# Sliding-window attention with a gated MLP on one core: scores of three units in one tiling mode at the head of an exp phase, first masks as products, second q,k pieces issued early

## The chip, the cores and the metric

The kernel runs on one NeuronCore of one Trainium2 chip. The time is device time in microseconds (us) of that core. Before the change it is 304.06 us, the median of five runs (302.56 to 306.17).

## What is computed

Eight batches of eight heads, 576 tokens, head size 64. A query sees itself and the 127 tokens before it; each head subtracts its own slope times the distance from the scores (ALiBi). The result, as 4608 rows of 512, goes through two matrices with g = h * cos(h) between them.

```python
scores = scale * np.matmul(q, k.transpose(0, 1, 3, 2))
slopes = 2.0 ** (-8.0 * (np.arange(H, dtype=np.float32) + 1) / H)
bias = slopes[:, None, None] * (-np.abs(rel).astype(np.float32))[None, :, :]
mask = (rel >= 0) & (rel < window)
scores = np.where(mask, scores + bias[None], -1000000000.0)
...
return np.matmul(attn, v).astype(np.float32)
...
h = x @ w_in
g = h * np.cos(h)
return (g @ w_out).astype(np.float32)
```

Scale is 1/8, window 128, H is 8; attn is the softmax of the scores along the keys. x has 512 columns, w_in goes to 2048 and w_out back to 512.

## The kernel before

**Units.** Attention is cut into units. A unit (b, pr, G) is a pair of heads pr (of four) of batch b and 256 queries (G = 0 or 1); (b, "t", None) is the rest of 64 queries for all eight heads. A batch has nine units, all have 72. For a unit, TensorE (PE) makes the scores with 64 rows of the array for each of the two heads side by side (`scores`), ScalarE (ACT) takes the exponential out of PSUM (`exps`, L538, for tails L530), VectorE (DVE) multiplies by the mask, exp(slope * distance) inside the window and 0 outside (`mask`, L562 and L549, from the tile EM, that `masks` makes on ACT, L431, from the distances `dif`), PE multiplies by v with a column of ones for the sums (`pv`, L593 and L596, for tails L580 and L582), DVE divides (`norm`, one unit, L632 and L634; `norm_two`, two units at once, L647 and L649), and the result is transposed into xT, the input of the first matrix: on PE (`x_pe`, L700; `x_pe_two`, L662; a copy by ACT or DVE after it) or, if it is needed only after the next chunk, by a DMA of the SP queue (`x_dma`). `norm_two` is used where the two units of a group are neighbours in pr at an even count of units.

**Chunks.** The MLP goes over nine chunks c of 512 rows. `moe1` makes h in 16 pieces, each four matmuls into one PSUM bank (L738; for chunk 0 halves, `moe1_half`, L762), a cosine on ACT (L744) and a product on DVE (L748). `moe2` multiplies by w_out: for chunk 0 plainly (L823), for the others as seven products of half-size blocks with sums in place of the eighth (L879), whose results ACT and DVE take out of the banks (L899, L903). Cosine and exponential need different tables on ACT, so a stage alternates: cosines of chunk c, then an exp phase with the units of the quota of c, beside which PE runs moe2 of c.

**PSUM.** Eight banks: SB, banks 4 to 7, for scores in two slots of two; UB, banks 2 and 3, for PV; OB, banks 0 and 1, for moe2. While units remain, moe1 takes the six banks of UB + SB in turn. QUOTA says how many units each exp phase has; the first nine units go before chunk 0. `attention` takes units in groups of two. In the phases the scores of a group are one op (with `mode=1`), in the first attention each unit has its own. PV follows by group.

**Order.** `Plan.op` records every operation with what it reads and writes; waits between engines follow from that. The order on each engine is not found at run time: STARTS is a packed table with a start for every op and, for copies that either may do, the choice of ACT or DVE. `schedule` sorts by it. POOL's ops keep the order in which the program names them: its queue carries the loads that convert to bf16 (q and k, v, w_in, w_out), and `identity` and `distances` run on the same engine. A new table can therefore reorder all engines but POOL.

**Start.** The first pieces of q (SP queue, then a cast on DVE and ACT, L321 and L322) and k (POOL) cover the first 256 tokens, the second pieces (`load_qk("q", q, 0, 1)` and the same for k) the rest. `qk_transposes` brings them into place on PE (L451) with copies on ACT and DVE (L468, L469). `warm` and `keep` are matmuls whose results nobody reads (L416, L424). w_in comes in four quarters; unit f2 of `moe1_half` reads quarter f2 // 2.

The softmax here doesn't subtract the row's maximum and nothing guards it: scores larger than these inputs give would overflow.

## Time and profile before

The profiled execution took 302.56 us, its span from the first to the last instruction is 300.8 us. It is the fastest of the five.

| engine | busy us | share of the span | largest groups (line, count, us busy) |
|---|---|---|---|
| PE | 293.6 | 98% | L738 x576, 130.9; L879, four groups, 155.0 in sum |
| DVE | 244.3 | 81% | L748 x128, 83.0; L562 x96, 41.9; L634 x36, 14.3; L649 x14, 9.7 |
| ACT | 210.2 | 70% | L744 x128, 82.4; L538 x64, 55.6 |
| POOL | 94.9 | 32% | loads of v (L329 x40), q and k (L339 x60) |

Further rows that the prediction uses, as mean duration of one:

| row | count | mean ns |
|---|---|---|
| L506 and L497, scores (PE) | 320 and 128 | 239 and 191 |
| L632 and L634, reciprocal and product of one unit (DVE) | 36 each | 171 and 419 |
| L647 and L649, the same of two units (DVE) | 14 each | 205 and 690 |
| L662 and L700, transposes of x (PE) | 20 and 50 | 219 and 220 |
| L431, masks (ACT) | 8 | 403 |
| L468 and L469, copies of transposed q and k (ACT, DVE) | 8 and 8 | 754 and 779 |
| L899, copy of a product out of PSUM (ACT) | 18 into qrows | 550 |

How to read it: a matmul's duration holds its way through the array, and the next one starts long before it ends; what one costs is the step from its start to the next start. A group's idle time stands before its instructions, with what ended it. Landings of loads are those of their semaphores in the trace.

### The profile page before, as it was taken

The numbers are of one execution on the slowest core, as the hardware profiler recorded it, in microseconds if no ns is written. First come the engines' busy times: TensorE is split into PE (matmuls) and PEld (weight loads), VectorE is DVE, ScalarE is ACT, GpSimd is POOL, SyncE is SP. The second block draws the span as 40 slices with busy tenths as digits, with TensorE's granted clock in tenths as the row PEclk, the third lists the DMA queues.
The fourth block names the chain that finished last, engine by engine and source line by source line (L and its number), as shares of the span: only waits on it lengthen the run. The fifth ranks groups of instructions, "written<-read, shape, count | busy, mean of one in ns | idle before, by whom it ended". The sixth has DMA issues, their size and how long they took to land.

```text
span 300.8 us, 7152 instructions
## 1 busy us (share of the span) xinstructions
PE 293.6 (98%) x2917; PEld 199.7 (66%) x2917; DVE 244.3 (81%) x511; ACT 210.2 (70%) x304; POOL 94.9 (32%) x122
## 2 busy tenths in 40 slices
PE   7789999999999999999999999999999999999996
PEld 3478745546874588547898886468655865666685
DVE  3787898679977998899978989899887966886871
ACT  6877777487877686787768866788567955745431
POOL 6930992059958401870195014000000000000000
DMA  7999999999999999999599999747014004310123
GB/s 138 180 200 211 207 171 145 143 141 225 157 137 205 158 156 187 171 169 159 91 141 136 135 114 137 144 79 124 11 53 117 9 2 113 107 35 2 35 87 124
DMA packets 148064, 38.02 MB, mean 126 GB/s; under 512 B 133696, under 2 KB 146752, under 8 KB 148032
## 3 DMA queue, kind: packets, MB, share of 16 engines
q0 software_dynamic: 99344, 18.10, 76.5%
q1 hardware_dynamic: 48688, 19.47, 33.4%
q8 instruction: 23, 0.38, 0.5%
q14 instruction: 9, 0.07, 0.1%
HBM read 36.70 MB, written 9.44 MB: 153 GB/s over the span
## 4 chain that ended last, share of the span: by engine, by line
PE 92%; DMA 4%; POOL 1%; issue 1%; DVE 0%; ACT 0%; ACTq 0%
PE ps L738 37%; PE ps L879 33%; PE ps L823 5%; PE ps L506 5%; PE ps L762 4%; DMA w_inb<-in_moe_w_in_dram 3%; PE ps L593 3%; PE ps L596 2%; DMA ob<-in_q_dram 1%; POOL vp L329 1%; PE ps L451 1%; PE ps L497 1%; PE ps L700 1%; PE ps L580 1%; PE ps L582 1%
## 5 line engine op out<-in xcount | busy, mean ns | idle before, releaser
L738 PE MATMUL ps<-xT,w_inb 128*128 128x512 bf16 (+1 forms) x576 | 130.9, 355 | 0.0
L744 ACT ACTIVATE cos<-ps,halfpi 128x512 f32<-128x512 f32 x128 | 82.4, 688 | 39.9 <-PE ps L738 24.2
L748 DVE TENSOR_TENSOR gT<-ps,cos 128x512 f16<-128x512 f32 x128 | 83.0, 686 | 21.4 <-ACT cos L744 20.3
L738 PEld LDWEIGHTS ps<-xT,w_inb 128*128 128x128 bf16 x576 | 55.2, 98 | 39.7 <-DVE gT L748 2.0
L538 ACT ACTIVATE p<-ps 128x768 bf16<-128x768 f32 (+1 forms) x64 | 55.6, 915 | 10.9 <-PE ps L506 8.2
L329 POOL DMA_DIRECT2D vp<-in_v_dram x40 | 33.9, 880 | 67.8 <-PE ps L596 52.0
L879 PE MATMUL ps<-wsum,gT 128*128 128x256 f16 x256 | 48.8, 273 | 0.0
L562 DVE TENSOR_TENSOR p<-p,emask 128x512 bf16<-128x512 bf16 (+2 forms) x96 | 41.9, 460 | 3.5 <-ACT p L538 2.9
L879 PE MATMUL ps<-w_outb,gT 128*128 128x256 f16 x256 | 41.8, 273 | 0.0
L879 PE MATMUL ps<-wsum,gsum 128*128 128x256 f16 x256 | 38.2, 273 | 0.0
L339 POOL DMA_DIRECT2D qnat<-in_q_dram x30 | 25.4, 888 | 16.6 <-DMA qt<-qnat 16.0
L879 PEld LDWEIGHTS ps<-w_outb,gT 128*128 128x128 f16 x256 | 24.6, 98 | 8.3 <-issue 0.5
L879 PEld LDWEIGHTS ps<-wsum,gT 128*128 128x128 f16 x256 | 24.2, 98 | 7.3 <-issue 0.6
L879 PEld LDWEIGHTS ps<-wsum,gsum 128*128 128x128 f16 x256 | 24.5, 98 | 5.2 <-DVE ob L903 0.2
L339 POOL DMA_DIRECT2D knat<-in_k_dram x30 | 25.5, 918 | 5.1 <-issue 4.3
L879 PE MATMUL ps<-w_outb,gsum 128*128 128x256 f16 x128 | 26.2, 273 | 0.0
L506 PE MATMUL ps<-qt,kt 64*128 64x128 bf16 (+1 forms) x320 | 18.8, 239 | 0.9 <-DVE kt L469 0.6
L593 PEld LDWEIGHTS ps<-vp,p 128*128 128x128 bf16 x256 | 16.2, 98 | 5.0 <-issue 1.9
L593 PE MATMUL ps<-vp,p 128*128 128x65 bf16 x256 | 18.3, 193 | 0.9 <-DVE p L562 0.8
L899 ACT ACTIVATE qrows<-ps 128x512 f32<-128x512 f32 (+1 forms) x18 | 9.9, 550 | 12.3 <-PE ps L879 12.2
L596 PE MATMUL ps<-vp,p 128*128 128x65 bf16 x192 | 17.1, 193 | 0.0
L823 PE MATMUL ps<-w_outb,gT 128*128 128x512 f16 x64 | 16.9, 380 | 0.0
(80 smaller groups left out, 339.8 us busy)
## 6 DMA issues: line engine op xcount, KB each, us to landing
out_dram<-ob SPq DMA_DIRECT2D x32, 256.0 KB, 3.0
vp<-in_v_dram POOLq DMA_DIRECT2D x32, 128.0 KB, 8.5
qnat<-in_q_dram POOLq DMA_DIRECT2D x24, 128.0 KB, 10.2
knat<-in_k_dram POOLq DMA_DIRECT2D x24, 128.0 KB, 12.8
w_inb<-in_moe_w_in_dram POOLq DMA_DIRECT2D x4, 512.0 KB, 9.8
w_outb<-in_moe_w_out_dram POOLq DMA_DIRECT2D x4, 512.0 KB, 21.2
out_dram<-ob SPq DMA_DIRECT2D x8, 128.0 KB, 1.7
qrows<-in_q_dram POOLq DMA_DIRECT2D x1, 576.0 KB, 14.5
```

The costliest lines, as they stand in the source:

```text
L329: op("pool", [lambda e, t=t, rows=rows: e.dma_start(vp[b % 2][0:rows, t, :, 0:64], v[b, :, 128 * t:128 * t + rows, :].rearrange("h p d -> ...
L339: fns.append(lambda e, t=t, rows=rows: e.dma_start(nat[which][b % 2][0:rows, t, :, :], src[b, :, 128 * t:128 * t + rows, :].rearrange("h p ...
L506: ins = e.matmul(ps[:, banks[x], c0:c1], keys_ap(b, x, pr, kc), query_ap(b, x, pr, qb, 128 * nb), start=True, stop=True)
L538: op("act", lambda e: e.activation(P[i][:, :, 0:hi], src_[:, :, 0:hi], ACTF.Exp, scale=0.125), w=held + [("P", i)], occ=920 if G else 691, ...
L562: op("dve", lambda e, p=p, m=m: e.tensor_tensor(p, p, m, ALU.mult), r=[("P", i), ("EM", h0), ("EM", h1)], w=[("P", i)] if n != 1 else [("P ...
L593: ins = e.matmul(o, P[i][:, x, d0:d0 + 128], V[:, kc, h, 0:65], start=True, stop=not two)
L596: ins = e.matmul(o, P[i][:, x, p0:p0 + 128], V[:, kc - 1, h, 0:65], start=False, stop=True)
L738: op("pe", lambda e, kc=kc, c0=c0: e.matmul(ps[:, bank, c0:c0 + n], w_in[:, kc, 128 * fc:128 * fc + 128], xT[:, kc, (r0 + c0) % XR:(r0 + c ...
L744: op("act", lambda e: e.activation(cosb[ci][:, :], ps[:, bank, :], ACTF.Sin, bias=halfpi[:, 0:1]), r=["halfpi"], w=[("B", bank), ("cos", c ...
L748: op("dve", lambda e: e.tensor_tensor(gT[gi][:, fc, :], ps[:, bank, :], cosb[ci][:, :], ALU.mult), r=[("cos", ci)], w=[("B", bank), ("g", ...
L823: op("pe", lambda e, t=t, fc=fc, bank=bank: e.matmul(ps[:, bank, :], gT[gi][:, fc, 128 * t:128 * t + 128], w_out[:, fc, :], start=(fc == 0 ...
L879: op("pe", lambda e, t=t, fc=fc, bk=bk: e.matmul(ps[:, bk, 256 * t:256 * t + 256], lhs(fc, t), rhs(fc), start=first and fc == 0 and (last ...
```

## The change

Six things in one diff, and a new table STARTS, which is left out here.

- `scores` takes a list of bank pairs instead of a slot number. A third slot, UB, is added to the two of SB. In an exp phase with an odd number of units the first group has three units, whose scores are one op; later groups have two.
- `attention` keeps units whose scores are made in a list `waiting` and hands them to PV (`attend`) as neighbours (pr even, pr + 1) also across groups.
- QUOTA moves one unit from the fifth phase to the fourth, so all phases have an odd number.
- For the four units of G = 0 in the first attention, `biases` puts 8 * slope * distance into the banks by matmuls of a scaled identity with `dif`; the scores add to it, and the mask multiplication of these units goes. The eight scaled identities are made on DVE and lie in output buffer 2. `dif` becomes bf16.
- The second pieces of q and k are issued on POOL before `identity` and `distances`, whose order is swapped.
- `keep` has a count of 0, and the two `warm2` matmuls go.

```diff
@@ -262,15 +261,16 @@
         NOB = 4
         obuf = sb("ob", [128, NOB, 512], F32)
         ob = [obuf[:, i, :] for i in range(NOB)]
+        scaled = obuf[:, 2, :].bitcast(BF16).rearrange("p (h c) -> p h c", h=H)
         rec = [sb(f"rec{i}", [128, 8], F32) for i in range(2)]
         ident = sb("ident", [128, 128])
         halfpi = sb("halfpi", [128, 1], F32)
-        dif = sb("dif", [128, 2, 128], F32)
+        dif = sb("dif", [128, 2, 128])
 
         ps = ctx.enter_context(nc.psum_tensor("ps", [128, 8, 512], F32))
         BPE = 2
-        KEEP = 4
-        QUOTA = [9, 9, 11, 10, 10, 9, 5]
+        KEEP = 0
+        QUOTA = [9, 9, 11, 11, 9, 9, 5]
         SB, UB, OB = [4, 5, 6, 7], [2, 3], [0, 1]
 
         slopes = [2.0 ** (-8.0 * (h + 1) / H) for h in range(H)]
@@ -425,6 +425,36 @@
                     ps[:, OB[0], :], EM[:, 0, 0:128],
                     EM[:, 0:2, :].rearrange("p h c -> p (h c)"), start=True, stop=True),
                    r=[("EM", 0), ("EM", 1)], w=[("B", OB[0])], occ=213, lat=378, pri=0)
+
+        def scaled_identities():
+            for h in range(H):
+                op("dve", lambda e, h=h: e.tensor_scalar(
+                    scaled[:, h, :], ident[:, :], 8.0 * slopes[h], None, ALU.mult),
+                   r=["ident"], w=[("scaled", h)], occ=95, lat=180, pri=3)
+
+        def biases(u, banks):
+
+            b, pr, G = u
+
+            def f(e):
+                ins = None
+                if pr == "t":
+                    for k_ in range(NPAIR):
+                        for x in range(2):
+                            ins = e.matmul(ps[:, banks[x], 128 * k_:128 * k_ + 128],
+                                           scaled[:, 2 * k_ + x, :], dif[:, :, 0:64],
+                                           start=k_ == 0, stop=False, skip_group_check=True)
+                    return ins
+                for c0, n in ((0, 2), (256, 2 if G else 1)):
+                    for x in range(2):
+                        ins = e.matmul(ps[:, banks[x], c0:c0 + 128 * n], scaled[:, 2 * pr + x, :],
+                                       dif[:, 0:n, :], start=c0 == 0, stop=False,
+                                       skip_group_check=True)
+                return ins
+            heads = range(H) if pr == "t" else (2 * pr, 2 * pr + 1)
+            occ = 460 if pr == "t" else 435 if G else 330
+            op("pe", f, r=["dif", ("ob", 2)] + [("scaled", h) for h in heads], w=[("B", x) for x in banks],
+               occ=occ, lat=occ + 165, pri=2)
 
         def masks():
             for h in range(H):
@@ -483,12 +513,13 @@
         def units(b):
             return [(b, pr, G) for G in range(2) for pr in range(NPAIR)] + [(b, "t", None)]
 
-        def scores(us, slot):
+        SLOTS = [SB[0:2], SB[2:4], UB]
+
+        def scores(us, slots, added=False):
 
             def f(e):
                 ins = None
-                for n, (b, pr, G) in enumerate(us, slot):
-                    banks = SB[2 * n:2 * n + 2]
+                for banks, (b, pr, G) in zip(slots, us):
                     if pr == "t":
                         for pr in range(NPAIR):
                             for half in range(2):
@@ -496,7 +527,8 @@
                                     c0 = 128 * pr + 64 * half
                                     ins = e.matmul(ps[:, banks[x], c0:c0 + 64],
                                                    keys_ap(b, x, pr, 4 - half),
-                                                   query_ap(b, x, pr, 4, 64), start=True, stop=True)
+                                                   query_ap(b, x, pr, 4, 64), start=not added, stop=True,
+                                                   skip_group_check=added)
                         continue
                     jobs = [(0, 256, 2 * G, 2 * G, 2), (256, 384, 2 * G + 1, 2 * G + 1, 1)]
                     if G:
@@ -504,23 +536,21 @@
                     for (c0, c1, kc, qb, nb) in jobs:
                         for x in range(2):
                             ins = e.matmul(ps[:, banks[x], c0:c1], keys_ap(b, x, pr, kc),
-                                           query_ap(b, x, pr, qb, 128 * nb), start=True, stop=True)
+                                           query_ap(b, x, pr, qb, 128 * nb), start=not added, stop=True,
+                                           skip_group_check=added)
                 return ins
             keys, held, occ = [], [], 0
-            for n, (b, pr, G) in enumerate(us, slot):
+            for banks, (b, pr, G) in zip(slots, us):
                 keys += tkeys((b, pr, G))
-                held += [("B", x) for x in SB[2 * n:2 * n + 2]]
+                held += [("B", x) for x in banks]
                 occ += 250 if pr == "t" else 220 if G else 165
-            if us[0] == (0, 0, 0):
-                keys.append("warm2")
             op("pe", f, r=keys, w=held, occ=occ, lat=occ + 165, mode=1, pri=2)
 
         pcount = {"P": 0, "Pt": 0}
         pbuf = {}
 
-        def exps(u, n, table):
+        def exps(u, banks, table):
             b, pr, G = u
-            banks = SB[2 * n:2 * n + 2]
             held = [("B", x) for x in banks]
             src_ = ps[:, banks[0]:banks[0] + 2, :]
             if pr == "t":
@@ -936,61 +966,82 @@
         SINGLE = False
         ucount = [0]
 
-        def attention(us, phase):
-
+        def attend(set_, phase):
+
+            pv(set_)
+            after = []
+            (b, pr, G), _ = set_[0]
+            if (phase >= 0 and len(set_) == 2 and set_[1][0] == (b, pr + 1, G)
+                    and ucount[0] % 2 == 0):
+                n = ucount[0]
+                ucount[0] += 2
+                norm_two(set_, n)
+                if (S * b + 256 * G) // CH > phase + 1:
+                    x_dma(set_[0][0], n)
+                    x_dma(set_[1][0], n + 1)
+                else:
+                    x_pe_two(set_, n)
+                return
+            for u, ub in set_:
+                n = ucount[0]
+                ucount[0] += 1
+                norm(u, ub, n)
+                first = (S * u[0] + (512 if u[1] == "t" else 256 * u[2])) // CH
+                after.append((first > phase + 1, u, ub, n))
+            for by_dma, u, ub, n in after:
+                if by_dma:
+                    x_dma(u, n)
+                else:
+                    x_pe(u, ub, n)
+
+        def first_attention(us):
             for g in range(0, len(us), 2):
                 two = us[g:g + 2]
-                if phase < 0 or SINGLE:
-                    for n, u in enumerate(two):
-                        scores([u], n)
-                        exps(u, n, 2 * phase + 2)
+                for n, u in enumerate(two):
+                    if u[2] == 0:
+                        biases(u, SLOTS[n])
+                    scores([u], [SLOTS[n]], u[2] == 0)
+                    exps(u, SLOTS[n], 0)
+                    if u[2] != 0:
                         mask(u)
-                else:
-                    scores(two, 0)
-                    for n, u in enumerate(two):
-                        exps(u, n, 2 * phase + 2)
-                    for u in two:
-                        mask(u)
-                if phase < 0 and g == 0:
-                    keep()
-                sets = [list(zip(two, OB if phase < 0 and g == 0 else UB))]
-                if any(u[1] == "t" for u in two):
-                    sets = [[s] for s in sets[0]]
-                for set_ in sets:
-                    pv(set_)
-                    after = []
-                    (b, pr, G), _ = set_[0]
-                    if (PAIRN and phase >= 0 and len(set_) == 2 and set_[1][0] == (b, pr + 1, G) and set_[0][1] == UB[0]
-                            and ucount[0] % 2 == 0):
-                        n = ucount[0]
-                        ucount[0] += 2
-                        norm_two(set_, n)
-                        if (S * b + 256 * G) // CH > phase + 1:
-                            x_dma(set_[0][0], n)
-                            x_dma(set_[1][0], n + 1)
-                        else:
-                            x_pe_two(set_, n)
-                        continue
-                    for u, ub in set_:
-                        n = ucount[0]
+                set_ = list(zip(two, UB if g else OB))
+                for each in [[s] for s in set_] if any(u[1] == "t" for u in two) else [set_]:
+                    attend(each, -1)
+
+        def attention(us, phase):
+
+            waiting, at = [], 0
+            while at < len(us):
+                size = 3 if at == 0 and len(us) % 2 else 2
+                group = us[at:at + size]
+                at += size
+                slots = ([UB] if size == 3 else []) + SLOTS[0:2]
+                scores(group, slots)
+                for u, banks in zip(group, slots):
+                    exps(u, banks, 2 * phase + 2)
+                for u in group:
+                    mask(u)
+                waiting += group
+                while waiting:
+                    b, pr, G = waiting[0]
+                    pair = pr != "t" and pr % 2 == 0
+                    if pair and len(waiting) < 2 and us[at:at + 1] == [(b, pr + 1, G)]:
+                        break
+                    pair = pair and waiting[1:2] == [(b, pr + 1, G)]
+                    if pair and ucount[0] % 2:
                         ucount[0] += 1
-                        norm(u, ub, n)
-                        first = (S * u[0] + (512 if u[1] == "t" else 256 * u[2])) // CH
-                        after.append((first > phase + 1, u, ub, n))
-                    for by_dma, u, ub, n in after:
-                        if by_dma:
-                            x_dma(u, n)
-                        else:
-                            x_pe(u, ub, n)
+                    attend(list(zip(waiting[:1 + pair], UB)), phase)
+                    waiting = waiting[1 + pair:]
 
 
         load_first_q()
         warm(9, 512, "warm")
         load_qk("k", k, 0, 0)
-        distances()
-        identity()
         load_qk("q", q, 0, 1)
         load_qk("k", k, 0, 1)
+        identity()
+        distances()
+        scaled_identities()
         constants()
         load_v(0, range(2))
         load_w_in(0)
@@ -999,8 +1050,6 @@
         for n in range(2):
             qk_transposes(0, "q", n, 0, OB)
             qk_transposes(0, "k", n, 0, UB)
-            if n == 0:
-                warm(2, 384, "warm2")
         for u in range(1, 4):
             load_w_in(u)
         load_qk("q", q, 1)
@@ -1010,7 +1059,7 @@
         load_v(1)
         weight_sums()
         every = [u for b in range(B) for u in units(b)]
-        attention(every[0:9], -1)
+        first_attention(every[0:9])
         done = 9
         next_t = 2
         for c in range(NCH):
```

## The prediction

> **What bounds the kernel now.** First the page: busy shares, the 40 slices, the chain of the work that ended last.
>
> ```profile
> PE 293.6 (98%) x2917; PEld 199.7 (66%) x2917; DVE 244.3 (81%) x511; ACT 210.2 (70%) x304; POOL 94.9 (32%) x122
> ...
> PE   7789999999999999999999999999999999999996
> ...
> DMA  7999999999999999999599999747014004310123
> ...
> PE 92%; DMA 4%; POOL 1%; issue 1%; DVE 0%; ACT 0%; ACTq 0%
> ```
>
> TensorE (PE) is busy 98% and carries 92% of the chain; only the first three slices (7, 7, 8 tenths) show holes. Busy is not peak, so I ask next for windows of the middle, and of the end of the start-up.
>
> ```profile
> 14.00:20.00 6.00, 5.18 (x84) 3.62 (x82) 5.61 (x20) 5.97 (x9) 3.76 (x6) 1.00 1.65 190
> ...
> 55.00:285.00 230.00, 229.87 (x2190) 155.92 (x2187) 195.04 (x393) 164.88 (x232) 62.84 (x75) 1.00 1.06 116
> ```
>
> From 55 to 285 us PE is busy for 229.87 of 230 us: nothing done on ACT, DVE, POOL or the queues in that stretch can shorten it. Only less PE time can: fewer columns, or less loss between matmuls. So I read PE's timeline of one stage for lost spacing.
>
> ```profile
> 135.92 2.02 PE L879 MATMUL ps<-w_outb,gT 128*128 128x256 f16 x17
> 137.87 0.50 PE L506 MATMUL ps<-qt,kt 64*128 64x256 bf16 x8
> 138.31 1.05 PE L879 MATMUL ps<-w_outb,gT 128*128 128x256 f16 x8
> ...
> 141.58 0.61 PE L506 MATMUL ps<-qt,kt 64*128 64x256 bf16 x12
> 142.13 0.50 PE L879 MATMUL ps<-wsum,gsum 128*128 128x256 f16 x3
> ```
>
> Columns are start, length, line, shapes, count; a length holds the modelled end of the last matmul. Seventeen L879 matmuls take 2.02 us with an end of 0.27, so they start every (2.02 - 0.27)/16 = 0.109 us. The last one's slot ends at 135.92 + 17 x 0.109 = 137.78; the scores (L506) start at 137.87, **0.09 us late**. The scores are 4 matmuls of 256 and 4 of 128 columns, two row halves side by side: 768 column times, at 0.109 per 256 that is 0.33 us. They hold PE from 137.87 to 138.31, 0.44 us: **0.11 us more**. The next stretch: 1024 column times are 0.44 us, PE is held for 142.13 - 141.58 = 0.55, again 0.11 more. One visit to the score mode costs about 0.20 us, whatever the number of units in it.
>
> Now the start. The chain of waits there:
>
> ```profile
> 11.16 8.86 DMA w_inb<-in_moe_w_in_dram
> ...
> 20.07 1.05 PE ps L762 x8
> ```
>
> PE takes up unbroken work at 20.07 us, when the second quarter of w_in has landed (issued at 11.16 us, 8.86 us in flight). Whether its DMAs are slow or late is read from windows of 1 us (last two columns: DMA share, GB/s):
>
> ```profile
> 4.00:5.00 1.00, 1.00 (x3) 0.15 (x1) 0.20 (x1) 0.76 (x3) 1.00 (x3) 1.00 1.20 256
> 5.00:6.00 1.00, 0.80 (x11) 0.52 (x12) 0.68 (x4) 1.00 (x4) 0.42 (x1) 1.00 1.43 148
> 6.00:7.00 1.00, 1.00 (x29) 0.86 (x24) 0.72 (x3) 1.00 (x4) 0.74 (x1) 1.00 0.86 120
> 7.00:8.00 1.00, 0.40 (x4) 0.09 (x4) 0.80 (x2) 0.92 (x3) 1.00 (x2) 1.00 1.13 179
> ...
> 12.00:13.00 1.00, 0.94 (x21) 0.73 (x22) 0.62 (x4) 0.78 (x2) 1.00 (x2) 1.00 1.23 206
> ```
>
> After the first pieces of q and k there is a dip at 5 to 7 us (148 and 120 GB/s between 256 and 179); afterwards it runs near 200 without a pause, so what is gained ahead of w_in reaches its landing. Last, what the first attention waits for:
>
> ```profile
> 9.16 0.43 DVE L562 TENSOR_TENSOR p<-p,emask 128x512 bf16<-128x512 bf16 x1 [1.37 <-ACT p L538]
> ...
> 12.20 0.16 PEld L593 LDWEIGHTS ps<-vp,p 128*128 128x128 bf16 x3 [0.53 <-issue]
> ...
> 13.19 2.85 ACT L538 ACTIVATE p<-ps 128x1024 bf16<-128x1024 f32 x3 [0.41 <-DVE p L562]
> ```
>
> Exps (ACT), masks (DVE), PV (PE) run one after another; PV begins at 12.20 us, just after v's second block has landed (12.14), so it too hangs on the stream. ACT is busy 5.97 of 6 us in 14 to 20 us.
>
> **What the Trainium skill says.** (1) *TensorEngine Tiling (Array Packing)*, Key Properties: changing the tiling mode, not just the tile, drains TensorE. The trace agrees: 0.09 us in, 0.11 us out. (2) *DMA: Bandwidth & Descriptors*, Queues, rings and completion order: each DMA engine takes the descriptors of a ring in order; so a piece issued earlier on POOL moves all behind it. The trace agrees: the POOL queue's loads land in the order of issue, krows 5.99, qrows 8.65, krows 10.41, v from 11.31, w_in 14.72 and 20.02 us. (3) *TensorE: Matmul & The Clock Gate*, Part 1: PE runs at half rate until it has been busy for about 3.4 us, and after an idle window again. The nine L416 warm-ups show the slow rate: 4.02 us for nine of 512 columns, 0.43 apart, where L424 later has (1.04 - 0.38)/3 = 0.22. (4) *SBUF — State Buffer*, Who interferes with whom: a DVE operation in a two-port mode and GpSimd block one another. No row of before shows that.
>
> **Part by part.**
>
> *Score groups.* Quotas 9,9,11,10,10,9,5 in twos are 5+5+6+5+5+5+3 = 34 stretches; 9,9,11,11,9,9,5 with a three at the head are 4+4+5+5+4+4+2 = 28. Columns stay. 6 x 0.20 = **-1.2 us**, all on PE, which has no cover in 55 to 285. One op issues all three units, so the stretch cannot come apart. Bounds: 0.6 (half falls beside other waits) to 1.3. New wait: the head's scores need banks 2 and 3 too, with all of moe2 queued behind them on PE. In the old loop moe1 fills the six banks in turn, so units 12 and 13 of 16 left these two, and 14 and 15 the ones the scores waited for already: the wait ends no later, zero. Its PV waits for the exp of the unit in its bank, whose result it reads anyway.
>
> *Pairs across groups.* Working through both loops: 14 double and 28 single norms become 28 doubles; units transposed on PE (x_pe) go from 17 + 2x5 = 27 to 2x13 = 26, by DMA from 29 to 30. One unit is 2 matmuls of 128 columns, 0.055 each: **-0.1 us** of PE; the one DMA more (2.4 us to landing) goes to SP. DVE falls by 28 x (0.171 + 0.419) - 14 x (0.205 + 0.690) = 4.0 us: zero, since PE covers DVE all through that stretch. If PE ever waits there, these are a small reserve. Unit (5,3,0) moves a stage forward; its batch's last transpose landed at 138.5, the scores of that batch come after 147: zero.
>
> *Second q,k pieces early.* On POOL they pass iota, two selects (1.25 us from 2.25 to 3.50) and the identity (0.56): q is issued near 2.15 instead of 3.95 us. The dip closes: 5 to 7 us lacked (200 - 148) + (200 - 120) = 132 KB, at 200 GB/s **-0.6 us** for v and w_in, thus for the 20.07. What they pass gets later: the identity ends near 4.2 (needed at 5.48, after q's cast: zero), dif near 5.2 instead of 3.5, so ACT's eight mask exps (L431; four take 1.32 us, so 0.31 apart) start later; three or four of them (0.9 to 1.2 us) move behind 8 us, where ACT is full. The POOL order behind them stays, v waits for DVE's memsets as now (0.84 us); if these come sooner, no gain counted, as the stream is full by then. Bounds: 0 to -0.85.
>
> *First masks as products.* Out: 8 masks L562 on DVE (four of about 0.42, four of 0.28: 2.8 us), four L424 (1.04 us) and two L416 (0.50 us) on PE. In: 16 matmuls, 3072 columns, 3072/256 x 0.109 = 1.3 us PE, up to four mode changes (0.8), and eight DVE scalings of 128x128 bf16. No row has these: at least 0.085 (the smallest memset), at most 0.19 (estimate from *VectorE: DVE Perf Modes*, its fixed 150 cycles and 4x mode: (150 + 32)/0.96); I take 0.1, so 0.8 us, in DVE's idle time before q's cast at 4.80. Were POOL locked out for the upper 1.5 us, v and w_in would lose up to that; range only. The products add a wait for dif and the scalings, with the first scores and all of PE behind them; both are there by about 5.5 us, the scores come at 7.94: zero. The scalings lie in output buffer 2, first stored from in the L823 stage after 34 us: zero. PE: the products of two units (0.65 us) fit where PE waits 0.60 us for kt before 7.94 and ran L416 for 0.50. DVE's 2.8 us can take over copies that ACT does now (L468 at 9.72 and 11.24, 0.89 each), against ACT's 0.9 to 1.2 of late mask exps; and the exp at 13.19 loses its wait of 0.41 for PV. So the attention ends roughly 0.5 to 1.5 us earlier. That only counts as far as PE work moves ahead of w_in's landing: the PV of two units at about 21 us (16 pairs, 0.5 us) and of the tail at 27.8 (0.5 us). I take one: **-0.5 us**; bounds +2.0 (late mask exps delay the second half of xT, PE runs dry before w_in's third quarter) to -2.0.
>
> Late next: w_in's third and fourth quarters (22.57, 25.52 us), which move with the stream.
>
> **Sum.** -1.2 - 0.1 - 0.6 - 0.5 = -2.4 us. The profiled execution has a span of 300.8 and took 302.56, 1.76 around it; so 300.2 for its like. It is the lowest of the five; the median is 304.06, 1.5 above. Forecast for the median: 304.06 - 2.4 = **301.7 us**.
>
> **Rivals.** *B, only the score mode pays:* the stream or ACT's late masks eat the start-up; -1.3 gives 302.8. For it: ACT is full until 18.5 us. *C, the start-up pays fully:* -0.85 and -2.0 with the 1.3 give 299.9. For it: 14 to 20 us has PE 5.18 of 6 with modelled ends in it. *D, slower:* at the head of each exp phase a third exp, 0.75 us after the second, stands before the copy of a product bank (L899), which PE needs for its third product after that; with six banks held by scores PE has nothing else. 7 phases x 0.75 = 5.3 us, less 2.4: +2.9, 307.0. It decides from 2.4/7 = 0.34 us per phase. Against it:
>
> ```profile
> 139.78 1.51 ACT L538 ACTIVATE p<-ps 128x768 bf16<-128x768 f32 x2
> 141.57 0.60 ACT L899 ACTIVATE qrows<-ps 128x512 f32<-128x512 f32 x1 [0.29 <-PE ps L879]
> ```
>
> the copy was waiting for PE (0.29 us), not PE for it, and its place in ACT's order is free.
>
> **Chances.** A (301.7, by itself 300.4 to 303.0) 0.55, B 0.15, C 0.15, D 0.15. Under 1%, 3.0 us, a measurement of this kernel cannot tell. Faster than 301.0: C nearly whole and a quarter of A, 0.28; slower than 307.1: most of D, 0.09; the rest 0.63. The range 299.8 to 304.8 leaves out most of D and a little of C.
>
> **What would show it.** L506 and L497 in 28 visits after 23 us, each with 0.09 before and 0.11 after; no dip at 5 to 7 us, w_in's second quarter near 19.4; PE unbroken from there; 28 doubles at L649; PE still full in 55 to 285. Wrong if PE waits for ACT's copies at a phase's head, if the first xT comes later than 17.4 us, or if the first matmuls show 0.43 spacing after 8 us.

## The result, and the profile after

Before: 304.04 us, the median of 80 executions (302.47 to 308.14). After: **304.23 us**, the median of 43 (302.81 to 308.12). Ratio 1.0005, 95% interval 0.9992 to 1.0018: no change that can be measured. The profiled execution after took 303.30 us, its span is 301.6. Both traces, of before and of after, are thus of executions faster than their kernel's median, by 1.5 and 0.9 us.

In the views of the changed kernel the lines have other numbers: L538 and L528 are the scores (L506 and L497 before), L792 the first products with w_in (L762), L909 moe2 (L879), L568 the exps (L538), and L431 is now a scaled identity, no longer a mask. The page after, busy time, slices of PE and DMA, and the chain of the work that ended last:

```profile
PE 292.6 (97%) x2925; PEld 200.6 (67%) x2925; DVE 241.2 (80%) x481; ACT 207.4 (69%) x297; POOL 95.2 (32%) x122
...
PE   7769999999999999999999999999999999999996
...
DMA  7999999999999999999999999942330014200223
...
PE 92%; DMA 6%; issue 1%; POOL 1%; DVE 0%; ACT 0%; DVEq 0%; ACTq 0%; POOLq 0%
```

PE has 1.0 us less to do, as meant. But its third slice fell from 8 to 6 tenths, and DMA's share of the chain rose from 4% to 6%: something was won later and lost in the first 23 us. First what was won, in PE's timeline of the fourth exp phase:

```profile
137.34 2.02 PE L909 MATMUL ps<-w_outb,gT 128*128 128x256 f16 x17
139.29 0.72 PE L538 MATMUL ps<-qt,kt 64*128 64x256 bf16 x14
139.94 0.61 PE L909 MATMUL ps<-w_outb,gT 128*128 128x256 f16 x4
```

Three units (fourteen matmuls, 1280 column times, 0.545 us) are one visit: 0.10 us after the last L909's slot has ended (137.34 + 17 x 0.109 = 139.19), and 0.65 held, 0.105 more than the columns. A visit costs what it did, and there are 28 after 23 us where there were 34. Summed over all start-to-start steps from 23 to 285 us, what PE loses beyond its columns (at 0.109 us per 256) is 9.15 us, before 10.06: **0.9 us won**. The same sum up to 23 us is 10.01, before 8.50: **1.5 us lost**. Windows of that stretch and of the middle (engines PE, PEld, DVE, ACT, POOL; then clock, DMA share, GB/s):

```profile
10.00:11.00 1.00, 0.60 (x20) 0.59 (x20) 1.00 (x2) 0.42 (x1) 1.00 (x2) 1.00 1.54 98
11.00:12.00 1.00, 1.00 (x16) 0.62 (x11) 0.98 (x2) 0.81 (x2) 1.00 (x3) 1.00 1.45 94
12.00:13.00 1.00, 0.73 (x14) 0.42 (x13) 0.06 (x1) 1.00 (x3) 1.00 (x2) 1.00 1.11 134
...
55.00:285.00 230.00, 229.77 (x2201) 156.35 (x2199) 193.83 (x370) 161.68 (x226) 62.86 (x75) 1.00 1.15 114
```

The middle is as full as before. But in 10 to 13 us the loads run at 98, 94 and 134 GB/s; before it was 155, 189 and 206. The chain shows what hangs on that:

```profile
11.84 9.90 DMA w_inb<-in_moe_w_in_dram
...
21.79 1.37 PE ps L792 x11
```

PE takes up the products with w_in's second quarter at 21.79 instead of 20.07 us. In the table of waits "PE ps L762 <- DMA w_inb" (0.3 us before) has become

```profile
PE ps L792 <- DMA w_inb<-in_moe_w_in_dram: 2.3, 2, 1.3
```

(us in total, times, longest). The longer of the two, 1.34 us up to 17.64, is for w_in's first quarter, which landed at 17.60 instead of 14.72 us; the other, 0.91 us up to 21.79, is for the second (21.75 instead of 20.02). Before, PE came to its first w_in product only at 17.41, when the first quarter was long there; the new order comes to it at 16.30 and has less room for a late one. Why the loads thin out is seen on POOL, which issues them, and on DVE. Before:

```profile
6.26 1.76 POOL L329 DMA_DIRECT2D vp<-in_v_dram  x2 [0.84 <-DVE vp L395]
```

After, POOL's row and DVE's work ahead of it:

```profile
6.89 1.81 POOL L329 DMA_DIRECT2D vp<-in_v_dram  x2 [1.35 <-DVE vp L395]
```

```profile
4.96 0.43 DVE L321 CAST qrows<-ob 128x512 bf16<-128x512 f32 x1 [3.60 <-DMA ob<-in_q_dram]
5.30 0.48 DVE L431 TENSOR_SCALAR ob<-ident 128x128 bf16<-128x128 bf16 x3
5.88 0.09 DVE L394 MEMSET vp<- 128x40 bf16 x1
...
6.01 0.22 DVE L431 TENSOR_SCALAR ob<-ident 128x128 bf16<-128x128 bf16 x2
6.33 0.27 DVE L395 MEMSET vp<- 64x256 uint32 x1
```

v's loads wait for two memsets of its buffer (L394, L395). Five of the new scalings now stand ahead of the last of these, which begins at 6.33 instead of 5.68 us (0.16 us of this is q's cast, which began at 4.96 instead of 4.80). So v is issued 0.63 us later; and q's and k's second pieces, issued at 2.16 and 2.88 instead of 3.95 and 4.70 us, no longer stand just before it in the stream. They landed no sooner for it: 8.75 and 10.36 us, before 8.65 and 10.41.

### The profile page after: what moved, and what is told of

It reads as the page before. It is cut to its first block, busy times and chain, and to the rows that moved or that the text cites. A ratio compares the mean times of both kernels' runs of the same rounds, so it can differ in the third digit from the quotient of the medians.

```text
span 301.6 us, 7136 instructions
## 1 busy us (share of the span) xinstructions
PE 292.6 (97%) x2925; PEld 200.6 (67%) x2925; DVE 241.2 (80%) x481; ACT 207.4 (69%) x297; POOL 95.2 (32%) x122
## 4 chain that ended last, share of the span: by engine, by line
PE 92%; DMA 6%; issue 1%; POOL 1%; DVE 0%; ACT 0%; DVEq 0%; ACTq 0%; POOLq 0%
PE ps L768 37%; PE ps L909 33%; PE ps L853 5%; PE ps L538 5%; PE ps L792 4%; DMA w_inb<-in_moe_w_in_dram 3%; PE ps L623 3%; DMA krows<-in_k_dram 2%; PE ps L626 2%; PE ps L481 1%; PE ps L692 1%; PE ps L610 1%; PE ps L612 1%; PE ps L528 1%; POOL krows L310 0%
## 5 line engine op out<-in xcount | busy, mean ns | idle before, releaser
L568 ACT ACTIVATE p<-ps 128x768 bf16<-128x768 f32 (+1 forms) x64 | 55.5, 917 | 7.0 <-PE ps L538 5.2
L909 PE MATMUL ps<-wsum,gT 128*128 128x256 f16 x256 | 50.1, 273 | 0.0
L909 PE MATMUL ps<-w_outb,gT 128*128 128x256 f16 x256 | 40.0, 273 | 0.0
L592 DVE TENSOR_TENSOR p<-p,emask 128x512 bf16<-128x512 bf16 (+2 forms) x88 | 38.7, 470 | 1.3 <-ACT p L568 1.0
L909 PE MATMUL ps<-wsum,gsum 128*128 128x256 f16 x256 | 38.0, 273 | 0.2 <-DVE ob L933 0.2
L909 PEld LDWEIGHTS ps<-wsum,gT 128*128 128x128 f16 x256 | 24.3, 98 | 8.5 <-issue 0.5
L909 PEld LDWEIGHTS ps<-w_outb,gT 128*128 128x128 f16 x256 | 24.5, 98 | 8.0 <-issue 0.3
L909 PEld LDWEIGHTS ps<-wsum,gsum 128*128 128x128 f16 x256 | 24.6, 98 | 5.2 <-DVE ob L933 0.4
L909 PE MATMUL ps<-w_outb,gsum 128*128 128x256 f16 x128 | 26.3, 273 | 0.0
L679 DVE TENSOR_TENSOR xnat<-ps,rec 128x512 bf16<-128x512 f32 x28 | 19.4, 691 | 1.9 <-DMA xT<-xnat 0.4
L538 PE MATMUL ps<-qt,kt 64*128 64x128 bf16 (+1 forms) x320 | 18.4, 239 | 0.7 <-DVE kt L499 0.7
L623 PE MATMUL ps<-vp,p 128*128 128x65 bf16 x256 | 17.9, 193 | 0.3 <-issue 0.3
L792 PE MATMUL ps<-xT,w_inb 128*128 128x256 bf16 x128 | 16.0, 273 | 2.3 <-DMA w_inb<-in_moe_w_in_dram 2.3
```

Of the source, the lines that this page charges most:

```text
L538: ins = e.matmul(ps[:, banks[x], c0:c1], keys_ap(b, x, pr, kc), query_ap(b, x, pr, qb, 128 * nb), start=not added, stop=True, skip_group_c ...
L568: op("act", lambda e: e.activation(P[i][:, :, 0:hi], src_[:, :, 0:hi], ACTF.Exp, scale=0.125), w=held + [("P", i)], occ=920 if G else 691, ...
L592: op("dve", lambda e, p=p, m=m: e.tensor_tensor(p, p, m, ALU.mult), r=[("P", i), ("EM", h0), ("EM", h1)], w=[("P", i)] if n != 1 else [("P ...
L623: ins = e.matmul(o, P[i][:, x, d0:d0 + 128], V[:, kc, h, 0:65], start=True, stop=not two)
L679: op("dve", lambda e: e.tensor_tensor(o, U[:, :, :, 0:64], rv[:, :, :, None].broadcast_to([128, 2, 4, 64]), ALU.mult), r=[("rec", n // 2 % ...
L792: op("pe", lambda e, i=i, fc=fc, kc=kc: e.matmul(ps[:, bank, 256 * i:256 * i + 256], w_in[:, kc, 128 * fc:128 * fc + 128], xT[:, kc, r0:r0 ...
```

## Experiments

Theory 1: the scalings ahead of v's memsets, made worse by the early pieces, cost the start-up what the score groups win. Rivals: the groups bring nothing by themselves; or what was lost is the early pieces' doing; or a wait in the middle takes it back (theory X). The columns give the median with the number of executions, the ratio to the kernel before, executed beside it (medians of 303.84 to 304.31; the ratio is not exactly the quotient of the two medians), v's first issue and the landing of w_in's second quarter in the profiled execution.

| run | kernel | us (n) | ratio, 95% | v | w_in |
|---|---|---|---|---|---|
| | after | 304.23 (43) | 1.0005, 0.9992 to 1.0018 | 6.89 | 21.75 |
| e1 | after, again | 305.73 (1) | | 6.82 | 21.97 |
| e2, e12 | after, v's memsets first | 302.11 (7), 302.20 (6) | 0.9931, 0.9907 to 0.9956; 0.9907, 0.9875 to 0.9939 | 5.50 | 20.20, 19.45 |
| e8 | after, old POOL order | 303.58 (22) | 0.9990, 0.9970 to 1.0010 | 6.65 | 20.96 |
| e15 | after, both of these | 301.84 (8) | 0.9922, 0.9892 to 0.9951 | 5.42 | 19.73 |
| e5 | before, again | 302.91 (1) | | 6.26 | 20.29 |
| e3 | before, early pieces | 304.13 (22) | 1.0005, 0.9986 to 1.0024 | 6.79 | 21.42 |
| e6 | before, v's memsets first | 303.16 (22) | 0.9973, 0.9963 to 0.9984 | 5.41 | 20.17 |
| e7 | before, both of these | 303.28 (22) | 0.9972, 0.9956 to 0.9989 | 5.50 | 19.46 |
| e16 | before's start-up, after's groups | 302.56 (22) | 0.9957, 0.9938 to 0.9977 | 6.36 | 20.14 |
| e17 | e16, v's memsets first | 302.01 (8) | 0.9926, 0.9899 to 0.9954 | 5.42 | 19.77 |

**e1 and e5**, both kernels again, unchanged, for the form of the start-up.

> The changed kernel unchanged, for a second trace. Theory 1 (the late v: on POOL the first load of v waits for a memset of the v tile that DVE now does after the scalings, the stream of loads runs short at 10 to 13 us, and w_in's second quarter lands late): the same hole comes again, 90 to 140 GB/s in 10 to 13 us, and the second quarter of w_in lands at 21 to 22 us. Theory 2 (a disturbance of that one execution, or of DMA at large): no hole, landing near 20 us.

> The kernel before unchanged, for a second trace, since its first was of the fastest of its executions. If its start is steady: no hole at 10 to 13 us, w_in's second quarter at 20.0 us within 0.4. If its first trace was a lucky one (which would explain why the early pieces alone, landing at 21.42, cost nothing in the median): landing at 20.5 us or later.

The hole was there again in after (130 and 107 GB/s at 10 to 12 us) and not in before (155 and 175), and PE again lost 1.5 us more up to 23 us (10.24 against 8.76): it is no accident of one execution.

**e2**, v's memsets ahead of the scalings; the numbers are ops in the order in which the program records them:

```diff
+        [setattr(self.all[i], 'start', t) for i, t in {29: 45, 30: 46}.items()]
         self.order = sorted(self.all, key=lambda o: (o.start, o.seq))
```

> The changed kernel with the two memsets that v's first load waits for moved on DVE to 1.4 us, ahead of q's cast; all else in place. Theory 1: v is issued near 5.5 us instead of 6.89, no hole at 10 to 13 us, w_in's second quarter lands at 19 to 20 us instead of 21.75, and the time falls by 1.5 to 2.5 us against the changed kernel, to a ratio of 0.992 to 0.995 to the kernel before. Theory 2 (something else slows the stream, such as DVE's copies of q and k at 9.6 to 12 us): v is issued earlier, yet the second quarter still lands after 21 us, ratio 1.000 within 0.002.

0.7% faster than before. POOL's row, and the windows where the hole was:

```profile
5.50 1.81 POOL L329 DMA_DIRECT2D vp<-in_v_dram  x2 [0.15 <-issue]
```

```profile
10.00:11.00 1.00, 0.48 (x18) 0.32 (x12) 0.47 (x1) 0.25 (x1) 1.00 (x2) 1.00 1.94 163
11.00:12.00 1.00, 0.67 (x20) 0.59 (x20) 1.00 (x2) 0.00 (x0) 1.00 (x3) 1.00 1.25 176
```

v no longer waits for DVE, and the hole is gone. Theory 1 holds. But moved memsets could be worth as much to the kernel before, and the early pieces stand in the stream too.

**e3, e6, e7**: the kernel before with the early pieces (`{19: 78, 20: 79, 17: 80, 18: 81, 2: 136}`), with v's memsets first (`{21: 46, 22: 46}`), and with both. POOL follows the starts too, contrary to what is said above under Order: `schedule` sorts all engines alike.

> The kernel before with one part of the change alone: the second pieces of q and k on POOL ahead of identity and distances (and q's cast on ACT ahead of the first masks, so that it does not wait for the later distances). Theory 1: v is issued at 6.2 us as before, the dip at 5 to 7 us closes, w_in's second quarter lands at 19.3 to 20 us, ratio 0.997 to 1.000. Theory 3 (the early pieces themselves leave the stream short before v): a hole at 10 to 13 us here too, landing at 20.5 us or later, ratio 1.001 to 1.006.

> The kernel before with only the two memsets of the v tile moved to 1.4 us on DVE: v is issued near 5.5 us instead of 6.26. If the stream of loads is full behind the second pieces anyway: landing of w_in's second quarter near 20 us, ratio 0.999 to 1.001. If late v costs the kernel before too: landing at 19 to 19.6 us, ratio 0.996 to 0.998.

> The kernel before with the early second pieces and the early memsets together: the start of the better version without the rest of the change. Theory 1 (early pieces pay only when v follows at once): no hole, landing at 19 to 20.3 us, ratio 0.995 to 0.998. If the better version's gain comes from the first masks and the groups of three alone: ratio 0.999 to 1.001.

e3 has a hole of 102 GB/s at 10 to 11 us (q's first piece landed at 5.32, half a microsecond late, so v was late as well), yet its time is that of before. The early memsets bring 1.0 us by themselves (e6, 303.16 against 304.13 of the kernel before beside it; 0.8 by the ratio); the early pieces bring nothing beside them (e7 against e6), though w_in lands 0.7 us sooner. So of e2's gain a part is one that the kernel before had left lying; e2 stands another 1.2 us under e7.

**e8**, the changed kernel with the old order of POOL's queue, and **e15**, the same with v's memsets first:

```diff
+        [setattr(self.all[i], 'start', t) for i, t in
+            {18: 60, 19: 61, 20: 62, 16: 63, 17: 64, 14: 150, 15: 180}.items()]
```

> The changed kernel with the old POOL order (distances, identity, then the second pieces), the memsets still late. Theory 3 (early pieces followed by a late v empty the rings): no hole at 10 to 13 us although v is issued as late as 6.8 us, w_in's second quarter lands at 20 to 20.7 us, ratio 0.995 to 0.998. Theory 1 in its first form (late v alone does it): the hole stays, landing after 21 us, ratio 1.000 within 0.002.

> The changed kernel with v's memsets ahead of the scalings (as e2) and the old order of POOL's queue (as e8): the fourth corner beside the changed kernel, e2 and e8. If the late v alone costs the time, the early pieces being worth nothing by themselves (as e6 against e7), it stands within 0.1 per cent of e2: ratio 0.991 to 0.994, v issued at 5.4 to 5.7 us, w_in's second quarter landed at 20.0 to 20.4 us. If the early pieces bring their 0.6 us once v is not late, it is 0.6 us over e2: 0.994 to 0.996.

e8 still has a hole, of 77 GB/s at 11 to 12 us, and w_in's second quarter landed at 20.96: the late v makes a hole without the early pieces too, against theory 3. The four corners are 304.23 (after), 303.58 (e8), 302.1 (e2) and 301.84 us (e15). The late v costs 2.1 us with the early pieces and 1.7 without. The early pieces seem to cost 0.65 us with the late v (the intervals overlap); without it they are worth nothing, not the 0.6 us that e15's rival expected.

**e4**, the other way round: a matmul over the full array between the units of each score operation, 35 more visits.

```diff
-                for banks, (b, pr, G) in zip(slots, us):
+                for n, (banks, (b, pr, G)) in enumerate(zip(slots, us)):
+                    if n:
+                        e.matmul(ps[:, banks[0], 0:128], ident[:, :], ident[:, :],
+                                 start=True, stop=True)
```

> The changed kernel with a full-array matmul of 128 columns between the units of each score op in the exp phases: 35 more visits to the score mode (63 instead of 28), results unchanged. If a visit costs 0.20 us of PE time with no cover, the time rises by 35 x (0.20 + 0.055) = 8.9 us against the changed kernel (7.0 us for the visits); if the visits hide beside other waits, by no more than the 1.9 us of the matmuls themselves.

312.28 us (4 executions, ratio 1.0267, 1.0240 to 1.0294), 8.05 over after. Less the 35 matmuls themselves at 0.055, this is 0.175 us for a visit: six fewer are worth 1.05 us.

**e13, e14**: the groups alone. The ops of the changed kernel's steady state behind the first ops of the kernel before, with both tables of starts joined at the end of the first attention; e14 with ten slots of normalised rows.

> The steady state of the changed kernel (groups of three, pairs across groups, the new quota) behind the start-up of the kernel before: masks on VectorE for all first units, warming products, the old order of POOL's queue. By the prediction's terms this part alone is worth 1.2 to 1.3 us; by the 0.175 us a visit that e4 showed, 1.05. Theory A (the prediction): the start-up is as before (v issued at 6.3 us, w_in's second quarter landed at 20.0 to 20.3 us) and the part brings its 1.0 to 1.3 us: ratio 0.9955 to 0.997. Theory X (the pairs across groups bring a wait for a slot of normalised rows near 158 us, which gives it back): that wait is there with 1 us or more and the ratio is 0.998 to 1.001.

> As e13, with 10 slots of normalised rows in place of 8. Theory X: no wait for a slot near 158 us, 0.5 to 1.3 us under e13, ratio 0.995 to 0.997. Theory A: within 0.3 us of e13.

304.42 us (22, ratio 1.0001, 0.9976 to 1.0026) and 305.12 (14, ratio 1.0011, 0.9983 to 1.0038). Read by the ratio alone, this said that the groups bring nothing; but the wait near 158 us by which theory X explained that is in neither trace. The windows of e13 (clock third from the end) show that it doesn't answer the question:

```profile
17.00:18.00 1.00, 0.12 (x5) 0.15 (x6) 0.00 (x0) 1.00 (x2) 0.85 (x2) 1.00 1.38 204
18.00:19.00 1.00, 0.63 (x17) 0.43 (x15) 0.44 (x4) 0.98 (x2) 0.00 (x0) 0.87 1.24 204
19.00:20.00 1.00, 0.34 (x3) 0.34 (x4) 1.00 (x3) 0.45 (x1) 0.00 (x0) 0.50 1.24 208
20.00:21.00 1.00, 1.00 (x8) 0.76 (x6) 1.00 (x4) 0.00 (x0) 0.00 (x0) 0.50 1.24 204
```

At the join of the two tables PE waits for v (1.5 us) and for a row of DVE (1.0), and soon after its clock is granted at half. In 18 of 22 executions of e13 the mean granted clock was under 0.998; the other four have a median of 302.00 us.

**e16, e17**: as e13, but with the starts of before kept until its w_in products run, so that PE's order is that of before up to about 22 us and that of after from there; e17 with v's memsets first.

> As e13, but with the start-up of the kernel before kept, instruction for instruction on TensorE, up to about 22 us (in e13 TensorE's order at 15 to 20 us was another, it waited 1.5 us for v, and 18 of 22 executions had a granted TensorE clock under 0.998, against 13 of 37 of the kernel before). Theory A (the groups of three are worth 1.0 to 1.3 us by themselves): v issued at 6.3 us, no wait for v over 0.5 us, lower clocks no more frequent than in the kernel before, ratio 0.9955 to 0.997. Theory X (a wait for a slot near 158 us takes it back): that wait over 1 us, 0.999 to 1.001.

> e16 with v's two memsets first on VectorE, as e6 has them. If the groups and the early v add up, the ratio is e16's times e6's 0.9973: 0.993 to 0.9945 by theory A. What e2 and e15 (0.991 to 0.993) have beyond that is then the first masks as products. Theory X: 0.996 to 0.998.

e16 is 1.3 us under the kernel before beside it (303.84), e17 1.8. The groups bring what was forecast, when the start-up is left alone. And e17, which has the old first masks and the old pieces, stands within 0.2 us of e2, e12 and e15, which have the products: **the first masks as products bring no time**. On ACT, e15's trace has no gain from them either:

```profile
10.99 0.89 ACT L498 ACTIVATE kt<-ps 128x640 bf16<-128x640 bf16 x1 [1.15 <-PE ps L481]
...
13.41 2.87 ACT L568 ACTIVATE p<-ps 128x1024 bf16<-128x1024 f32 x3
```

With DVE's masks gone, ACT stands still for 1.15 us until k's second piece is there (landed at 10.15) and transposed; the row of full exps starts at 13.41, in before at 13.19. PE did get ahead for a while: it came to the scores of the first exp phase at 38.93 us, in e17 at 40.06. But then it met loads that were not earlier by as much:

```profile
PE ps L792 <- DMA w_inb<-in_moe_w_in_dram: 0.8, 1, 0.8
PE ps L853 <- DMA w_outb<-in_moe_w_out_dram: 0.4, 1, 0.4
```

The second wait is for w_out's last quarter (landed at 42.20), and at the third visit to the score mode, near 47 us, the lead is 0.4 us; from the third exp phase on it is 0.25 us or less. This is read from one trace of each kernel; no run took these waits away one by one.

**Theory X: e9, e10, e12, e14, e18.** In e1, e2, e8 and e12, PE waits 1.1 to 1.5 us near 158 us; not in the profile of after. DVE and PE in e12:

```profile
158.22 0.69 DVE L679 TENSOR_TENSOR xnat<-ps,rec 128x512 bf16<-128x512 f32 x1 [1.92 <-DMA xT<-xnat]
```

```profile
158.97 2.25 PE L768 MATMUL ps<-xT,w_inb 128*128 128x256 bf16 x19 [1.28 <-DVE xnat L679]
```

The last double norm of the phase needs a slot of normalised rows that a DMA transpose is still reading; DVE's next products, and by them PE, stand behind it. Ten slots instead of eight:

```diff
-        NX = 8
+        NX = 10
```

> The changed kernel with v's two memsets ahead of the scalings (as e2) and with 10 slots in place of 8 in the ring of normalised rows (xnat). Theory X (the products of the fourth phase's end, near 158 us, are late because the DVE work that fills a slot waits for the DMA transpose that still reads it): with two more slots no wait of PE on xnat's fill is left there, and 0.5 to 1.3 us go beside e2 of the same call: ratio 0.988 to 0.992. Rival (the slot is not what is late there: the transposes behind it, or DVE's own queue, take the place of it): PE waits as long near 158 us, ratio as e2's, 0.992 to 0.995.

> e2's kernel once more, on the same chip as e9 to e11, so that the two slots can be read against it: ratio 0.992 to 0.995 by the theory of the late memsets. If e2's gain was of its few runs or of its chip, 0.997 or more.

> The changed kernel with 10 slots in place of 8 in the ring of normalised rows, and nothing else. Theory X: the start-up is as in the changed kernel (v issued at 6.8 to 6.9 us, w_in's second quarter landed at 21.5 to 22 us), the wait near 158 us is gone: ratio 0.996 to 0.998. Rival: no difference to the changed kernel, 0.999 to 1.002.

> e17 with 10 slots of normalised rows in place of 8. Theory X: no wait of PE for a slot near 158 us, 0.5 to 1.3 us under e17. Theory A: within 0.3 us of e17.

The wait is in none of the traces with ten slots. The time doesn't follow: e9 302.64 us (6 executions, ratio 0.9930, 0.9904 to 0.9955) against e12's 302.20; e18 302.39 (19, ratio 0.9946, 0.9925 to 0.9966) against e17's 302.01, where the wait wasn't to be seen with eight slots either. Only e10, 303.75 (22, ratio 0.9982, 0.9965 to 0.9999), is below after's 1.0005, with intervals that overlap. The wait is real in some executions (the four profiled ones that have it took 0.6 to 2.3 us more than their kernels' medians); that it costs the median anything is not shown.

**e11**, e9 with w_in's second quarter issued ahead of v's last block (`64: 400` added).

> As e9, with the load of w_in's second quarter issued ahead of v's last block on POOL's queue. If the products of w_in at 18 to 22 us wait for the second quarter alone, it lands 0.5 to 1 us sooner and the time is 0.3 to 0.8 us under e9's (ratio 0.986 to 0.990). Rival (the bytes ahead of it are the same within a few per cent, or v's last block is then the late one): within 0.2 us of e9.

301.98 us (6, ratio 0.9910, 0.9884 to 0.9936), w_in landed at 19.01, and no wait for it is left. It is 0.66 us under e9, with intervals that overlap. e2, e11, e12, e15 and e17 beat both kernels; they can't be told from each other.

## Why the prediction was wrong

Forecast: 301.7 us; measured: 304.23. This lies within the stated range, but above what A and B gave (at most 303.0), in the part left to D, whose wait did not come: that the range holds it is luck. By the terms of the sum, along the kernels before (304.04), e16 (302.56), e8 (303.58) and after (304.23):

- **Score groups -1.2 and pairs -0.1: right.** e16 shows -1.3 (its ratio) or -1.5 (along the chain of medians), e4's price of a visit -1.05, the profile of after -0.9. 28 visits of 0.10 in and 0.105 out, and 28 double norms, were seen.
- **First masks as products -0.5: this is the step that failed,** and it is +1.0 (e8 less e16, the ends of whose intervals overlap a little; with v's memsets first, e15 less e17, it is -0.2). Three sentences of it did. "eight DVE scalings of 128x128 bf16 ... so 0.8 us, in DVE's idle time before q's cast at 4.80": they take 1.4 us (next row), one 0.213 instead of at most 0.19, and they start at 5.30, behind the cast, since the written order has them there although the identity is done at 4.17. "v waits for DVE's memsets as now (0.84 us)": it waits 1.35, because the scalings lie between the memsets. I had costed them on DVE, which has time, and not on POOL's queue, which waits for the memset behind them. And "the attention ends roughly 0.5 to 1.5 us earlier" left out what PE then meets: the exps of the second half need the second pieces, which land no sooner, and w_in and w_out come hardly sooner either. With v late, PE came to its first w_in product 1.1 us sooner and waited there 1.34 us for the first quarter; without the delay of v it was 1.1 us ahead of e17 at 39 us, and the gain in the time is still nil (e15 and e2 against e17).

```profile
L431 DVE TENSOR_SCALAR ob<-ident 128x128 bf16<-128x128 bf16 x8 | 1.4, 213 | 0.0
```

- **Second pieces early -0.6: wrong as well.** They were issued 1.8 us sooner, but they landed at the same time, and the dip at 5 to 7 us closed by half (171 and 159 GB/s). The pieces are worth nothing when v is on time (e7 against e6, e2 against e15) and seem to cost 0.65 us when it is not. The forecast counted room in the dip as gained for all that is behind; but v and w_in were issued later, not sooner, and when e2 and e7 mended that, the time still showed nothing of it. The stream behind the dip was not "near 200" throughout either: in before it ran at 155 to 211 GB/s from 7 to 17 us.
- **Costed at nothing:** DVE's savings were worth nothing, as said. Rival D, which makes the time longer by a third exp ahead of L899, did not happen: PE is busy 229.77 of 230 us. Rival B, "only the score mode pays", named the side of the error but not its size: the start-up didn't merely bring nothing, it took back what the groups had brought.

What the range had as "Were POOL locked out for the upper 1.5 us, v and w_in would lose up to that" is near the effect in size, but the cause is another: POOL waited for a semaphore. The Trainium skill's *DMA: Bandwidth & Descriptors*, Queues, rings and completion order, says of the queues of SP and ACT that each engine takes a ring's descriptors in order; POOL's loads keep the order here too (w_in's quarters land in the order of issue in all traces), and so what delays v's issue is felt by w_in behind it.

The version with v's memsets first does reach the forecast time, but in part by luck: 1.3 us of it are the groups, as forecast, and about 0.8 the earlier v (e6), for which the forecast had counted nothing.

**Open:** w_in's second quarter lands 1.7 us later for a v issued 0.6 us later; without the early pieces (e8) it is 0.9 us for 0.4, and how the delay grows is not explained. Why the late v costs the changed kernel 1.7 to 2.1 us and the kernel before about half of that was not tested; that the new order comes to w_in's first quarter a microsecond sooner is the likely reason. And the two profiled executions of before took 302.56 and 302.91 us, both at its low end; what its median execution loses beyond them was not traced, so e6's 1.0 us is a measured time without a place in a trace: w_in landed no sooner there. Of the 1.0, 0.67 is there among executions at full clock alone (303.16, 21 of them, against 303.83, 43; see the last section).

## What to carry to other kernels

An operation put on an engine with idle time isn't free if another queue waits for what stands behind it there: look for who waits on the engine's next instructions, and put the ones that release loads first (here two memsets, about 0.9 us in the kernel before and 2 us in the changed one). Work taken off one engine at the start is worth only what the next input allows; ask which load the freed engine will wait for. When two orders of work are joined for an experiment, look at the join in the trace before reading the time.

## What had not been expected of the hardware

The clock that PE is granted differs from execution to execution of one kernel. Of the 193 executions of the kernel before that stood beside these runs, 60 had a mean under 0.998; of after about a quarter; of e15 and e17 none of 16; of e13 18 of 22. The means lie near 0.994 and 0.989, which is one or two stretches of about 3.4 us at half rate in 300 (0.5 x 3.4/300 = 0.0057). In e14's windows the half rate lasts (1 - 0.72)/0.5 + 2 + (1 - 0.57)/0.5 = 3.4 us, after PE had stood still at 16.41 to 17.36 and 18.11 to 19.14 us; in e13's it is twice that. The Trainium skill, *TensorE: Matmul & The Clock Gate*, Part 1, says that the gate looks at free-running windows of 3413 ns; the lengths agree, and that the windows don't start with the kernel would be why only some executions are hit; no run here tests it. Such a stretch costs 1 to 2 us here (e13: 302.00 at full clock, 304.20 near 0.994, 305.51 near 0.989). A start-up with holes thus pays twice (e16, the same groups without e13's two holes: 5 of 22), and a part of each median above is how often that happens. It is not what sets the kernels apart: among executions with a mean of 0.998 or more alone the medians are 303.94 us for after, 303.13 for e8, 302.26 for e16, 302.01 for e17, 301.95 for e2 and 301.85 for e15, against 303.49 to 304.25 for the kernel before beside them.
